# Half-height TensorE tiles, one stretch for four pairs' last queries, and a new order in a funnel-attention and maxout kernel

## The chip, the cores and the metric

The kernel runs on one core of a Trainium2 chip. The metric is device time in microseconds; lower is better. Median of three runs before the change: 359.93 us (359.83 to 361.86).

## The reference

Attention over queries that are averaged in pairs, then a two-branch layer with a maximum:

```python
q_pool = q.reshape(B, H, S // 2, 2, D).mean(axis=3)         # B 8, H 8, S 1152, D 64
scores = scale * q_pool @ k.transpose(0, 1, 3, 2)
attn = exp(scores) / sum(exp(scores))
x = (attn @ v).transpose(0, 2, 1, 3).reshape(B * 576, 512)  # 4608 tokens
g = np.maximum(x @ w1, x @ w2)                              # 512 x 1024 each
out = g @ w_out                                             # 1024 x 512
```

Inputs and output are float32; the kernel multiplies in bf16.

## The kernel before

**The work.** The 64 heads are handled as 32 pairs (`NPAIR`), four to a batch. A pair has 9 x 576 columns of scores per head; all pairs' columns, one after the other, are cut into 324 groups of 512 (`scores`, `exps`). For a group TensorE makes the scores of both heads in 64-row tiles, one in the upper and one in the lower half of the array (line 290), and ScalarE takes the exp of 2 x 512 columns into `et` (line 305; where a group crosses a turn of the buffer, two exps, so 336 in all). K and Q must be transposed first: Q on TensorE (line 491) for pairs 0 to 4, on VectorE (line 446) after that; K on TensorE (line 512) for pairs 0 to 4, by a DMA transpose after that.

Attention times V (`av_jobs`): per head four blocks of 128 queries, each nine matmuls with a 128 x 128 weight tile (line 569), and 64 remaining queries in 128 x 64 tiles (line 584). The 64 of an even pair are copied to `rem` by POOL (`keep_rest`, line 429), so that two pairs' remainders run in one stretch. A column of ones in V yields the sums; VectorE divides (lines 598 to 606). The result x is transposed by DMA, or on TensorE for the pairs in `X_PE` (lines 660 and 663).

The second layer uses max(a, b) = relu(a - b) + b. So x(W1 - W2) goes through a relu (`h_jobs`, line 694; evicted at 705 or 709), and the output is that times Wo plus x(W2 Wo) (`p_job`, line 737; `z_job` at the end). W2 Wo is made once: W2 is cast, transposed on TensorE (`w2t_job`, line 530) and multiplied by Wo (`w21_job`, line 543), both in 128-row tiles. `fill` (line 473) multiplies ones by ones: 28 times before the first data are there, and later two at a time.

**What sets the order.** The order of all instructions is one string, written out: each symbol issues one step. `S` is a group of scores, `E` an exp, `A` a part of attention times V, `Q` and `K` transposes, `T` and `W` W2's transposes and its product with Wo, `X` transposes of x, `0` to `3` four running jobs of the second layer (the sequence `MOE`), `Z` its last rows, `F` two matmuls of ones; small letters are evictions, casts (`k`, `q`, `v`), copies of remainders (`e`), loads (`l`), DMA transposes (`t`, `x`) and stores (`o`). `BANKS` names the PSUM bank of each job. Every engine executes its own steps in the string's order; `Plan` adds the semaphore waits. TensorE's steps thus differ in tile size: 64-row (scores and second layer), 128 x 128 (`A`, `K`, `T`, `W`, `X`, `F`, `Z`), 128 x 64 (remainders), 64 x 64 (`Q`).

SyncE issues nearly all loads in the order `LOADS`, and the DMA transposes and stores between them. q, k and v have three buffers each. From exp 42 on a load also waits until the exp two before the last one issued is done (`pace`).

Of the kernel before, what the change touches and what calls it, by code (L numbers as in the profile page):

```python
# [5 lines left out]
FP32 = mybir.dt.float32  # L6
BF16 = mybir.dt.bfloat16
P = 128
# [108 lines left out]
def bass_funnel_attn__then__act_maxout2_kernel(  # L117
# [38 lines left out]
    W_CASTS = ((0, 1), (0, 2), (0, 0), (0, 3), (2, 0), (2, 1), (2, 2), (2, 3))  # L156
    W_DIFFS = ((0, 0), (0, 1), (3, 1), (1, 1), (1, 0), (3, 0), (2, 1), (2, 0))
    W_DIFFS_DVE = ()
    FILL = 28
    FILLS = 6  # L160
    PACE = 2
    PACE_FROM = 40
    LOADS = (
# [16 lines left out]
        "hhhhpphhhhpphhhhhhhhpphhhhpphhhhphhhhpphhhhphhhhphhhhpphhhhhphhhhphhh"  # L180
    )
    BANKS = (
        "0102346702674670602456042760460245602456012456214624160246246021460234064032646203460426704064036206"
        "2402642604264206250624024624624620742064064060560640640240260246124064024026412640240240240240246246"
        "2562462464267024602462062402462562624640646246246246246206206036026206260202612602402614262642042040"
        "4040645064064062416240204620642642674264240246240634062062462074206406406065060460240240240240202404"
        "2064306426046060467046064060640265026404024024012640260420460142604206406406420101420002406206204232"
# [3 lines left out]
    with ctx:  # L191
# [20 lines left out]
        rc = [sbuf([P, NCH + 2], FP32, f"rc{s}") for s in range(2)]  # L212
# [15 lines left out]
        osb = [osb2[:, s, :] for s in range(4)]  # L228

# [91 lines left out]
        done = [0]  # L321

        def load_k(i, lo=0, hi=NT, eng="SP"):
            b, h0, s = i // NHP, 2 * (i % NHP), i % 3
            op(eng, lambda e: e.dma_start(  # L325
                kraw[s][:, :, lo:hi, :].rearrange("p h t d -> p h (t d)"),
                k[b, h0:h0 + 2, :, :].rearrange("h (p t) d -> p h (t d)", t=NT)[
                    :, :, lo * D:hi * D]),
                after=([f"kraw0.{c}" for c in K0] if s == 0 and hi - lo == NT else []) + pace(),
                w=[f"kraw0.{lo}"] if hi - lo < NT else [f"kraw{s}"],  # L330
                dma=f"d_kp{lo}" if hi - lo < NT else f"d_k{s}",
                cost=1.45 * (hi - lo) / NT + (0.47 if lo == 6 else 0.0), tag=("L", "k", i))

        def load_q(i, lo=0, hi=QU, eng="SP"):
            b, h0, s = i // NHP, 2 * (i % NHP), i % 3
            op(eng, lambda e: e.dma_start(  # L336
# [3 lines left out]
                w=[f"qraw0.{lo}"] if hi - lo < QU else [f"qraw{s}"],  # L340
                after=(["qraw0.0", "qraw0.4"] if s == 0 and hi - lo == QU else []) + pace(),
                dma=f"d_qp{lo}" if hi - lo < QU else f"d_q{s}",
                cost=1.45 * (hi - lo) / QU + (1.1 if lo else 0.0), tag=("L", "q", i))

        def load_v(i):
            b, h0, s = i // NHP, 2 * (i % NHP), i % 3
            op("SP", lambda e: e.dma_start(
                vraw[s][:, :, :, :].rearrange("p h t d -> p h (t d)"),
                v[b, h0:h0 + 2, :, :].rearrange("h (p t) d -> p h (t d)", t=NT)),
                w=[f"vraw{s}"], after=pace(), dma=f"d_v{s}", cost=1.48, tag=("L", "v", i))  # L350

        def w_load(part, c):
            src, dst, name = ((moe_w2, w2f, "w2f"), (moe_w1, w1f, "w1f"), (moe_w_out, wof, "wof"))[part]
            n = 2 if part == 2 else 1
            op("SP", lambda e: e.dma_start(
                dst[:, c * n:(c + 1) * n, :],
                src.rearrange("(c p) f -> p c f", p=P)[:, c * n:(c + 1) * n, :]),
                w=[f"{name}{c}"], dma=f"d_w{part}{c}", cost=1.34, tag=("L", "w", part, c))
# [3 lines left out]
        def setup():  # L362
# [11 lines left out]
            if FILL:  # L374
                op("DVE", lambda e: e.memset(rem[:, 0, :, :], 1.0), w=["rem"], cost=0.1)
                op("PE", lambda e: fill(e, 7, FILL), r=["rem"], w=["b7"], cost=0.0563 * FILL, mode="f",
                   tag=("f0",))
# [37 lines left out]
        def cast_v(i):  # L415
            r = i % 3
            op("POOL", lambda g: g.tensor_scalar(  # L417
                vE[r][:, :, :, 0:D].rearrange("p t h d -> p h t d"), vraw[r][:, :, :, :],
                1.0, 1.0, ALU.mult, ALU.mult), r=[f"vraw{r}"], w=[f"vE{r}", f"v.{i}"], cost=1.154,
                tag=("cv", i))  # L420

        def keep_rest(i):
            a = flat(i, 0, NCH * P)
            step = flat(i, 1, NCH * P) - a
            base = (i % 2) * PW + a
            src = et2[:, :, base:base + NT * step].rearrange("p h (t c) -> p t h c", c=step)[:, :, :, 0:NB] \
                if base + NT * step <= 2 * PW else None
# [546 lines left out]
```

## Time and profile before

| | |
|---|---|
| median of 3 runs | 359.93 us |
| the profiled execution | 360.63 us |
| its span, first to last instruction | 358.9 us |
| TensorE busy | 349.2 us |
| ScalarE busy | 315.3 us, of it exps 303.8 |
| VectorE busy | 236.0 us |
| POOL busy | 143.4 us |
| granted TensorE clock | 1.00 |
| moved by DMA | 84.67 MB, 236 GB/s |

How to read it: PE is TensorE's matmuls, PEld its weight loads, DVE VectorE, ACT ScalarE, SP SyncE. In rows of groups stand line, engine, operation, output <- inputs, shape, count, then busy time in all and the mean of one in ns, then the engine's idle time ahead of them and what ended most of it. In rows in order of time stand start, length, engine, line and, in brackets, the idle time before. Rows of TensorE in order of time overlap, because each matmul's latency is in its length; the distance of two starts is what the first one takes from the stream. A tile is given as rows*columns, so 64*128 is a half-height tile.

### The profile page before, as it was taken

To read this page: it belongs to the slowest core of one execution; us is meant where nothing else is said; L and a number is where in the kernel's file an instruction comes from. 1 tells how busy PE (TensorE), PEld (TensorE's weight loads), DVE (VectorE), ACT (ScalarE), POOL (GpSimd) and SP (SyncE) were. 2 spreads that over 40 slices of the span, in tenths; PEclk is the share of its full clock that TensorE was granted. 3 is DMA by queue.
4 is the path that set the end of the run, shared out by engine and by line. 5 is a ranking of instruction groups with operands and counts; after the bars stand their busy time and mean duration, and the time that the engine had idled before them with its cause. 6 is when DMAs were issued, how large, how long until landed. Compare 5 with 4: busy or idle time off the path is not lost.

```text
span 358.9 us, 13458 instructions
## 1 busy us (share of the span) xinstructions
PE 349.2 (97%) x6009; PEld 218.0 (61%) x6009; DVE 236.0 (66%) x516; ACT 315.3 (88%) x355; POOL 143.4 (40%) x128
## 2 busy tenths in 40 slices
PE   7699999999999999999999999999999999999996
PEld 5465655655566675656664675666676655657663
DVE  3686578977798658976796776884787774514001
ACT  5999989999999989999999898999999898890431
POOL 2446997363645171744417152535425220100000
PEclk9999999999999999999999999999999999999999
DMA  8999999999999999998999989899999853002224
GB/s 264 409 392 395 316 374 257 298 244 291 314 244 315 288 294 297 329 260 148 343 209 301 233 217 305 187 274 255 196 265 228 170 113 75 17 23 59 60 60 117
DMA packets 77434, 84.67 MB, mean 236 GB/s; under 512 B 49216, under 2 KB 50496, under 8 KB 77376
## 3 DMA queue, kind: packets, MB, share of 16 engines
q1 hardware_dynamic: 76592, 83.28, 88.3%
q8 instruction: 47, 0.77, 0.9%
q10 hardware_dynamic: 784, 0.52, 0.5%
q14 instruction: 11, 0.09, 0.1%
HBM read 62.91 MB, written 9.44 MB: 202 GB/s over the span
## 4 chain that ended last, share of the span: by engine, by line
PE 92%; DMA 3%; ACT 2%; SPq 1%; issue 1%; DVE 0%
PE ps L737 25%; PE ps L290 21%; PE ps L569 21%; PE ps L694 18%; PE ps L584 3%; DMA qraw<-in_q_dram 3%; ACT et L305 2%; PE ps L543 2%; PE ps L780 1%; PE ps L660 1%; SPq L325 0%; PE ps L491 0%; PE ps L512 0%; SPq L336 0%; PE ps L663 0%
## 5 line engine op out<-in xcount | busy, mean ns | idle before, releaser
L305 ACT ACTIVATE et<-ps 128x1024 bf16<-128x1024 f32 (+1 forms) x336 | 303.8, 1016 | 14.0 <-PE ps L290 13.1
L290 PE MATMUL ps<-qpT,kT 64*128 64x256 bf16 (+7 forms) x1162 | 114.5, 283 | 1.2 <-DVE qpT L498 0.6
L446 DVE STREAM_TRANSPOSE qpT<-qp 32x288 bf16<-32x288 bf16 x216 | 101.4, 469 | 12.7 <-PE ps L290 6.0
L694 PE MATMUL ps<-xT,wd 64*128 64x512 bf16 (+3 forms) x832 | 84.1, 311 | 0.0
L569 PEld LDWEIGHTS ps<-vE,et 128*128 128x128 bf16 x2304 | 73.6, 97 | 16.9 <-issue 10.0
L569 PE MATMUL ps<-vE,et 128*128 128x65 bf16 x2304 | 81.5, 193 | 1.9 <-issue 1.4
L737 PE MATMUL ps<-wo,stage 64*128 64x512 bf16 x544 | 78.4, 376 | 0.0
L290 PEld LDWEIGHTS ps<-qpT,kT 64*128 64x128 bf16 x1162 | 47.6, 94 | 48.4 <-ACT et L305 15.1
L411 POOL TENSOR_TENSOR qp<-qraw 128x576 bf16<-128x576 f32 x30 | 42.1, 1406 | 53.8 <-DVE qpT L446 48.9
L417 POOL TENSOR_SCALAR vE<-vraw 128x1152 bf16<-128x1152 f32 x32 | 36.9, 1152 | 56.8 <-PE ps L584 39.3
L694 PEld LDWEIGHTS ps<-xT,wd 64*128 64x128 bf16 x832 | 36.0, 94 | 24.5 <-ACT et L305 1.7
L381 POOL TENSOR_SCALAR kbf<-kraw 128x1152 bf16<-128x1152 f32 x31 | 35.7, 1151 | 32.5 <-DMA kraw<-in_k_dram 24.6
L705 DVE TENSOR_SCALAR stage<-ps 128x1024 bf16<-128x1024 f32 (+3 forms) x40 | 39.1, 979 | 13.4 <-PE ps L694 12.7
L737 PE MATMUL ps<-w,xT 64*128 64x512 bf16 x272 | 39.9, 377 | 0.0
L737 PEld LDWEIGHTS ps<-wo,stage 64*128 64x128 bf16 x544 | 25.8, 94 | 18.5
L598 DVE RECIPROCAL rc<-ps 128x4 f32<-128x4 f32 (+1 forms) x64 | 11.8, 184 | 35.5 <-PE ps L569 34.9
L606 DVE TENSOR_TENSOR xnat<-ps,rc 128x256 bf16<-128x256 f32 x64 | 27.2, 424 | 1.9
L429 POOL TENSOR_SCALAR rem<-et 128x1152 bf16<-128x1152 bf16 x16 | 18.4, 1152 | 20.9 <-ACT et L305 20.8
L743 DVE COPY stage<-ps 128x1024 f32<-128x1024 f32 x14 | 17.0, 1216 | 11.6 <-PE ps L737 11.4
L709 ACT ACTIVATE stage<-ps 128x512 bf16<-128x512 f32 (+1 forms) x12 | 6.0, 525 | 17.4 <-PE ps L694 17.4
L785 DVE COPY stage<-ps 128x512 f32<-128x512 f32 (+1 forms) x2 | 1.0, 492 | 25.7 <-PE ps L780 25.7
L737 PEld LDWEIGHTS ps<-w,xT 64*128 64x128 bf16 x272 | 12.6, 94 | 8.5 <-ACT et L305 0.2
(46 smaller groups left out, 138.5 us busy)
## 6 DMA issues: line engine op xcount, KB each, us to landing
vraw<-in_v_dram SPq DMA_DIRECT2D x32, 576.0 KB, 6.1
kraw<-in_k_dram SPq DMA_DIRECT2D x31, 576.0 KB, 7.0
qraw<-in_q_dram SPq DMA_DIRECT2D x31, 576.0 KB, 6.2
out_dram<-stage SPq DMA_DIRECT2D x24, 256.0 KB, 3.8
out_dram<-stage SPq DMA_DIRECT2D x21, 128.0 KB, 3.0
xT<-in_moe_w_dram SPq DMA_DIRECT2D x4, 512.0 KB, 11.2
stage<-in_moe_w_out_dram SPq DMA_DIRECT2D x4, 512.0 KB, 13.6
stage<-in_moe_w_dram SPq DMA_DIRECT2D x4, 512.0 KB, 14.0
```

The lines of the kernel that those rows point to most:

```text
L290: last = e.matmul(ps[:, h, col:col + hi - lo], kT[i % 3][rows(h), t, :], qpT[i % 3][rows(h), lo:hi], start=True, stop=True)
L305: op("ACT", lambda e: e.activation(et2[:, :, c:c + z - a], ps[:, :, a - g * W:z - g * W], EXP, scale=scale), r=[f"b{m}", f"b{m + 1}"], w=w ...
L381: op("POOL", lambda g: g.tensor_scalar(kbf[s][:, :, :, :].rearrange("p t h d -> p h t d"), kraw[r][:, :, :, :], 1.0, 1.0, ALU.mult, ALU.mu ...
L411: op("POOL", lambda g: g.tensor_tensor(qpf[s][:, :, :], qraw[r][:, :, 0, :], qraw[r][:, :, 1, :], ALU.add), r=[f"qraw{r}"], w=[f"qp{s}.0", ...
L417: op("POOL", lambda g: g.tensor_scalar(vE[r][:, :, :, 0:D].rearrange("p t h d -> p h t d"), vraw[r][:, :, :, :], 1.0, 1.0, ALU.mult, ALU.m ...
L429: op("POOL", lambda g: g.tensor_scalar(rem[:, :, :, :], src, 1.0, 1.0, ALU.mult, ALU.mult), r=[f"et{i % 2}.{g - first(i)}" for g in range( ...
L446: op("DVE", lambda e: e.transpose(view[dst:dst + 32, :, 32 * pb:32 * pb + 32], qpf[s][src:src + 32, :, 32 * db:32 * db + 32]), r=[f"qp{s}. ...
L569: last = e.matmul(fb[m][:, sb * 66:sb * 66 + 65], et[:, a:a + P], vE[vs][:, t, half, 0:65], start=(t == 0), stop=(t == NT - 1))
L606: todo.append(evac_op("DVE", lambda e, m: e.tensor_tensor(xnat[xs][:, i % NHP, :, half * D:half * D + D], a(m)[:, 0:NCH, 0:D], rc[half][:, ...
L694: last = e.matmul(fb[m + k][:, 0:size], wd[z, ct, (f0 + k) * P:(f0 + k + 1) * P], xT[z, ct, n0:n1], start=(turn == 0 and ct == 0), stop=(t ...
L705: return e.tensor_scalar_max(gT[:, f0:f0 + 2, g0:g0 + size], wide[m // 2][:, :, 0:size], 0.0)
L737: last = e.matmul(fb[m + k][:, :], lhs, rhs, start=(turn == 0 and j == 0), stop=(turn == 1 and j == NC_ + NF - 1))
```

## The change

- K's transposes of pairs 0 to 4, W2's and those of x on TensorE: each 128 x 128 tile becomes two 64-row transposes in the two halves of the array, into two PSUM banks; the eviction reads both banks. K of pairs 1 to 4 is one job instead of two.
- W2 times Wo: two jobs of two column tiles in 64-row tiles, 64 matmuls of 512 columns in place of 32 in full tiles. They run as the first jobs of the second layer's sequence (`w` in `MOE`), with one eviction each.
- Remainders: from batch 1 on the four pairs of a batch in one stretch (`FOUR`). Three `rem` buffers and a fourth V buffer (in the space of loaded weights that are no longer needed); POOL copies three of four pairs; the last pair's jobs take three and five blocks of 128 queries; VectorE divides four remainders at once; one DMA transpose per four.
- Matmuls of ones: 16 pairs later on in place of 6 (`FILLS`).
- Loads: a new order, and SyncE's loads from the 15th on wait for the landing of the third load before (`BEHIND`).
- The order string, `BANKS`, `MOE` and the order of casts are new.

```diff
-    FILLS = 6
+    FILLS = 16
+    BEHIND = ((14, 3),)
+    FOUR = 1
...
-        ("q", 0, 4, 9), ("k", 1), ("w", 0, 1), ("k", 2), ("q", 1), ("v", 0), ("w", 0, 2), ("w", 0, 0),
-        ("q", 2), ("w", 0, 3), ("q", 3), ("v", 1), ("w", 2, 0), ("w", 2, 1), ("k", 3), ("w", 2, 2),
-        ("w", 2, 3), ("w", 1, 0), ("k", 4), ("q", 4), ("k", 5), ("v", 2), ("v", 3), ("w", 1, 3),
+        ("q", 0, 4, 9), ("k", 1), ("q", 1), ("q", 2), ("k", 2), ("v", 0), ("w", 0, 1), ("w", 0, 3),
+        ("k", 3), ("w", 0, 0), ("w", 0, 2), ("v", 1), ("w", 2, 0), ("w", 2, 1), ("w", 2, 2), ("q", 3),
+        ("w", 2, 3), ("w", 1, 3), ("v", 2), ("w", 1, 2), ("k", 4), ("w", 1, 1), ("q", 4), ("q", 5),
...
+        def behind():
+            n = issued[0]
+            issued[0] += 1
+            back = [d for at, d in BEHIND if at <= n]
+            return [f"ld{n - back[-1]}"] if back else [], [f"ld{n}"]
...
+        def halves(e, m, at, src):
+            for z in range(2):
+                mb = fb[m + z][:, :].bitcast(BF16)
+                last = e.transpose(mb[:, at:at + HP], src[rows(z), :], ident[rows(z), rows(z)])
+            return last
...
-                    last = e.transpose(
-                        mb[:, (t - lo) * P:(t - lo + 1) * P],
-                        kbf[s][:, t, :, :].rearrange("p h d -> p (h d)"), ident[:, :])
+                    last = halves(e, m, (t - lo) * HP, kbf[s][:, t, :, :].rearrange("p h d -> p (h d)"))
...
-                    return e.matmul(fb[m][:, :], w2T[:, ct, ft, :], wo[:, ft, :],
-                                    start=(ft == 0), stop=(ft == NF - 1))
+                    for k in range(2):
+                        z = rows(turn ^ k)
+                        last = e.matmul(fb[m + k][:, :], w2T[z, c0 + k, j, :], wo[z, j, :],
+                                        start=(turn == 0 and j == 0), stop=(turn == 1 and j == NF - 1))
...
+            n = 4 if i // NHP >= FOUR else 2
+            return [i + 1 - n + j for j in range(n)] if i % n == n - 1 else []
...
+            if len(ends) == NHP:
+                return [Job(("a", i, 0), 1, [rest(j, 3 + at) for at, j in enumerate(ends)]
+                            + [chunk(0, sb, sb) for sb in range(3)],
+                            norm(0, 7, [ending(0, 3), ending(1, 3), blocks(0, 0, 0, 3)])),
+                        Job(("a", i, 1), 1, [chunk(0, 3, 0)] + [chunk(1, sb, 1 + sb) for sb in range(NCH)],
+                            norm(1, 5, [blocks(0, 0, 3, 1), blocks(1, 1, 0, NCH)]))]
```

More of the change, by code (lines that the diff above doesn't have):

```diff
@@ new lines, in norm, with blocks, ending @@
+                return todo
+            def blocks(half, at, lo, num):
+                return (slice(0, P), at, num, xnat[xs][:, c, lo:lo + num, half * D:half * D + D],
+                        [f"xn{xs}.{h0 + half}"], 0.154 + 0.068 * num)
+            def ending(k, at):
+                c0 = ends[0] % NHP
+                return (rows(k), at, len(ends), xend[xs][rows(0), c0:c0 + len(ends), k * D:k * D + D],
+                        [f"xr{xs}.{2 * (j % NHP) + k}" for j in ends], 0.154 + 0.068 * len(ends))
@@ new lines, in av_jobs @@
+            if len(ends) == NHP:
[4 more added lines that the diff above has]
+                            norm(1, 5, [blocks(0, 0, 3, 1), blocks(1, 1, 0, NCH)]))]
+            lead = [rest(j, NCH + at) for at, j in enumerate(ends)]
@@ L616, in place @@
+            more = [ending(0, NCH), ending(1, NCH)] if ends else []
+            return [Job(("a", i, half), 1, (lead if half == 0 else [])
+                        + [chunk(half, sb, sb) for sb in range(NCH)],
+                        norm(half, NCH + (len(ends) if half == 0 else 0),
+                             (more if half == 0 else []) + [blocks(half, 0, 0, NCH)]))
+                    for half in range(2)]
         def place(b, j):
```

293 lines of the change are left out of this document (156 added, 137 removed), and 8 rows, old and new, of the table LOADS.

## The prediction

> **What bounds the kernel now.** I read the head of the page first, then the table by stages, then ScalarE's and TensorE's instructions in order of time.
>
> ```profile
> span 358.9 us, 13458 instructions
> PE 349.2 (97%) x6009; PEld 218.0 (61%) x6009; DVE 236.0 (66%) x516; ACT 315.3 (88%) x355; POOL 143.4 (40%) x128
> PE 92%; DMA 3%; ACT 2%; SPq 1%; issue 1%; DVE 0%
> ...
> 10.00:20.00 10.00, 7.46 (x156) 5.55 (x158) 7.77 (x14) 9.68 (x11) 4.93 (x5) 1.00 1.03 408
> 20.00:30.00 10.00, 9.53 (x191) 6.14 (x185) 9.24 (x17) 10.00 (x13) 4.16 (x4) 1.00 1.05 390
> 30.00:40.00 10.00, 9.98 (x118) 4.68 (x118) 4.96 (x12) 10.00 (x12) 8.38 (x7) 1.00 1.04 400
> 80.00:120.00 40.00, 40.00 (x708) 24.35 (x706) 31.06 (x70) 39.80 (x45) 19.31 (x17) 1.00 1.12 286
> 160.00:323.00 163.00, 163.00 (x2858) 101.69 (x2855) 112.24 (x242) 153.75 (x170) 56.63 (x47) 1.00 0.84 199
> ...
> 6.10 6.55 ACT L305 ACTIVATE et<-ps 128x1024 bf16<-128x1024 f32 x7 [0.89 <-PE ps L290]
> 12.88 36.31 ACT L305 ACTIVATE et<-ps 128x1024 bf16<-128x1024 f32 x41 [0.23 <-PE ps L290]
> 50.24 12.20 ACT L305 ACTIVATE et<-ps 128x1024 bf16<-128x1024 f32 x13 [1.05 <-PE ps L290]
> ```
>
> (Columns of the stages: length, busy time of PE, PEld, DVE, ACT, POOL, clock, DMA share, GB/s.) There are two regimes. From 6.10 to 49.2 us ScalarE runs 48 exps with one gap, 0.23 us: it sets the pace, and between 10 and 20 us TensorE is busy only 7.46 of 10. From 50 us on TensorE has no free time (163.00 of 163.00), while ScalarE gets some (153.75). So from exp 48, the 49th, the end is what TensorE still has to do. Ahead of it, shorter TensorE work only makes TensorE wait longer for exps.
>
> **What TensorE pays beside its columns.** The next rows are TensorE's, in the steady part.
>
> ```profile
> 203.07 0.38 PE L290 MATMUL ps<-qpT,kT 64*128 64x512 bf16 x2
> 203.29 1.03 PE L737 MATMUL ps<-wo,stage 64*128 64x512 bf16 x8
> 204.15 0.38 PE L290 MATMUL ps<-qpT,kT 64*128 64x512 bf16 x2
> 204.37 0.59 PE L737 MATMUL ps<-wo,stage 64*128 64x512 bf16 x4
> 204.89 0.47 PE L584 MATMUL ps<-vE,rem 128*64 128x65 bf16 x18
> ...
> 197.65 0.60 PE L290 MATMUL ps<-qpT,kT 64*128 64x128 bf16 x8
> 198.18 2.35 PE L569 MATMUL ps<-vE,et 128*128 128x65 bf16 x72
> 200.46 0.39 PE L290 MATMUL ps<-qpT,kT 64*128 64x256 bf16 x4
> ...
> 53.64 0.40 PE L660 MATMUL ps<-ident,xnat 128*128 128x128 bf16 x4
> 53.97 0.23 PE L663 MATMUL ps<-ident,xend 64*128 64x64 bf16 x2
> ```
>
> I use starts, since ends are pipelined. Where the tile size stays, a pair of 64-row matmuls of 512 columns takes 203.29 - 203.07 = 0.22 us. Four of them at 204.37 should take 0.43, but the next row starts 0.52 later, and its tiles are 128*64: the switch costs 0.09. Eight at 197.65 are two groups, 0.43; the 128*128 row comes 0.53 later: 0.10. Four transposes at 53.64 take 0.33 with their switch. I price a switch at 0.096 us, and the plain rates at 0.216 a 512-column slot, 0.056 a 128*128 transpose and 0.27 a nine-step attention block.
>
> **The change, part by part.** I walked both order strings, gave every TensorE symbol its tile size and counted the changes of size: 205 before, 172 after. That is 33 x 0.096 = 3.17 us less.
>
> ```profile
> L512 PE MATMUL ps<-ident,kbf 128*128 128x128 bf16 x45 | 4.4, 221 | 1.3 <-POOL kbf L381 0.9 <-ACT kbf L394 0.3
> L530 PE MATMUL ps<-ident,xT 128*128 128x128 bf16 x32 | 2.3, 220 | 0.6 <-DVE xT L454 0.6
> L660 PE MATMUL ps<-ident,xnat 128*128 128x128 bf16 x32 | 3.2, 221 | 0.0
> L663 PE MATMUL ps<-ident,xend 64*128 64x64 bf16 x12 | 1.4, 195 | 0.0
> L491 PE MATMUL ps<-ident,qp 64*64 64x64 bf16 x90 | 2.5, 195 | 0.5 <-DVE qp L404 0.5
> L543 PE MATMUL ps<-wo,xT 128*128 128x512 bf16 x32 | 9.0, 382 | 0.0
> 14.36 0.47 PE L491 MATMUL ps<-ident,qp 64*64 64x64 bf16 x18 [0.47 <-DVE qp L404]
> ```
>
> K, W2, x: 45 + 32 + 32 = 109 tiles of 0.056 become 109 pairs of 64-row transposes. No row has such a pair. The nearest, L491's 18 small ones, take 0.47 with 0.195 of latency, so 0.275 / 9 = 0.031 a pair. Bounds: 0.027 (64 columns at the 512-column rate), and 0.060 if the two halves do not overlap, since L569 above loads a full weight tile every (200.46 - 198.18 - 0.096) / 72 = 0.030. I take 0.030: -2.8 us. Eight more 64-query transposes of x on TensorE cost 8 x 0.03 = +0.2. W2 times Wo: 32 slots either way: 0. So TensorE's own work falls by 3.2 + 2.6 = 5.8 us; summed over the whole walk, with a half-tile pair near its lower bound, 334.6 becomes 328.5, 6.1 less.
>
> How much lies behind exp 48? Switches there: 142 before, 110 after, -3.07 us. Six W2Wo slots (6 x 0.216 = 1.30) move ahead of it; two attention blocks (+0.54) and one score group less (-0.21) come behind it; two more x transposes, each cheaper, are even. Sum: -4.0 to -4.1 us. The other 2.0 us, nearly all of the K and W2 transposes, lie where ScalarE sets the pace: worth 0.
>
> ```profile
> L584 PE MATMUL ps<-vE,rem 128*64 128x65 bf16 x288 | 7.6, 197 | 0.0
> L429 POOL TENSOR_SCALAR rem<-et 128x1152 bf16<-128x1152 bf16 x16 | 18.4, 1152 | 20.9 <-ACT et L305 20.8
> L602 DVE TENSOR_TENSOR xend<-ps,rc 64x64 bf16<-64x64 f32 x64 | 14.2, 221 | 1.2
> L519 DVE COPY kT<-ps 128x640 bf16<-128x640 bf16 x4 | 1.9, 483 | 0.5 <-PE ps L512 0.5
> L519 DVE COPY kT<-ps 128x512 bf16<-128x512 bf16 x4 | 1.7, 419 | 1.9 <-PE ps L512 1.9
> L473 PE MATMUL ps<-rem 128*128 128x128 bf16 x40 | 4.5, 290 | 1.1 <-DVE rem L375 1.1
> ```
>
> Last 64 queries of four pairs: as many L584 steps, in 13 stretches instead of 17 (its switches are counted). POOL copies 23 times instead of 16, 7 x 1.152 = 8 us, hidden while POOL is 40% busy. If POOL falls behind, the v cast behind the copy holds up attention. DVE's 64 L602 become 4 of twice and 14 of four times the width: some 5 us less, on no path. SyncE issues seven DMA transposes fewer. The evictions of the half-tiles write two strips: 0 if they keep L519's rate, (483 - 419 ns) / 128 elements by its two sizes; at twice that, nine tiles cost 0.6 us more five times, in a stage where DVE is 9.24 of 10 busy. Ten more pairs of matmuls of ones (20 x 0.056 = 1.1) fall into the idle 2.5 us between 10 and 20: 0; without that cover, 1.1.
>
> ```profile
> kraw<-in_k_dram SPq DMA_DIRECT2D x31, 576.0 KB, 7.0
> qraw<-in_q_dram SPq DMA_DIRECT2D x31, 576.0 KB, 6.2
> 4.20 9.32 DMA qraw<-in_q_dram
> ```
>
> Loads: each SyncE load from the 15th on waits until the one three before it has landed; stores and DMA transposes queue behind that wait. The transfers take 576 KB / 400 GB/s = 1.47 us each, so three cover 4.4 us of latency. At 7.0 us they would not; but the 7.0 contains queueing. I take a latency of 4.4 or less: 0. Weights are also moved ahead of q3 and q4. q1 landed at 4.20 + 9.32 = 13.52 with 3.47 MB through it; 9.57 MB stand up to q3 now, so q3 lands at 13.5 + 6.1 / 0.40 = 28.8, some 3 us of cast, transpose and eviction before its first exp at about 33; q4 10 us later, with some 1.5 us to spare. Pair 1's q comes earlier.
>
> **Sum.** The profiled execution took 360.63 us (span 358.9); the median of the runs shown is 359.93, 0.70 lower. 360.63 - 4.1 = 356.5. ScalarE is then even nearer to full between 50 and 120 (39.80 of 40 already), so I give back 0.2 of the bound of 1.05, the one wait of that kind in the rows: 356.7, or 356.0 as a median.
>
> **The rivals.** *All 6.1 us count,* because the early exps come sooner too: 353.8. For it, ScalarE's one early gap; against it, that gap is only 0.23.
>
> *Loads too late (the other side).* If three in flight take 7.0 us, a load takes 2.33 instead of 1.47: eleven loads from the 15th to q4 lose 9.5 us, less 1.5 to spare, 8.0: 364.0. It takes the whole gain of 4.1 from (4.1 + 1.5) / 11 = 0.51 us more a load, so from 2.0 us a load. For it, the 7.0; against it, that DMA moves 400 GB/s there whatever the queue holds.
>
> *Halves do not overlap:* 109 x 0.060 = 6.5 instead of 6.1 us; 77 of the tiles come early, when TensorE is 9.5 to 10 of 10 busy, so some 2 us: 358.0. [...] No run here shows two half-tile loads back to back.
>
> ```profile
> 10.57 0.68 PE L512 MATMUL ps<-ident,kbf 128*128 128x128 bf16 x9 [0.77 <-POOL kbf L381]
> 1.10 3.38 PE L473 MATMUL ps<-rem 128*128 128x128 bf16 x30 [1.10 <-DVE rem L375]
> ```
>
> *The clock falls.* TensorE idles more between 8 and 17 us, its W2 work being later. The first 30 matmuls of ones ran at (3.38 - 0.29) / 29 = 0.107 us each instead of 0.056. Another such stretch of 3.38 us at half rate costs up to 1.7 us: 357.7. The granted clock was 1.00 with 7.46 of 10 busy and gaps of up to 0.77 us, and the new matmuls of ones are spread over this stretch, which speaks against it. [...]
>
> **How the numbers follow.** My forecast 0.55 (own range 355 to 357.3), all counted 0.14, late loads 0.16, no overlap 0.09, clock 0.06. About 1%, 3.6 us, is what a measurement can tell from no change: faster means below 356.3. That takes 0.33 of my forecast's 0.55 and all of the second: 0.47. Late loads end above 363.5 with 0.12 of their 0.16. The rest, 0.41, is within 1%. The range 353.7 to 361.0 leaves out late loads beyond the point where they decide, and little below.
>
> **What would show it.** Right: switches of tile size down to about 172; row pairs of half-tile transposes starting about 0.03 us apart; ScalarE without gaps up to exp 48 and exp 48 at about 50; TensorE full from 50 us on. Wrong: gaps of ScalarE before exp 48 that end on a DMA or on a q or k cast; a clock below 1.00; transposes 0.06 apart; new TensorE waits after 50 us.

## The result, and the profile after

The changed kernel takes 363.74 us (median of 8 executions, 362.14 to 366.06) against 359.88 for the kernel before (8 executions): a ratio of 1.0089, interval 1.0061 to 1.0117. It is slower by 3.9 us by the medians (3.2 by the ratio) where 3.9 faster was forecast. The profiled execution took 362.49 us. In it, scores are L302 (before L290), exps L317 (L305), half-tile transposes of K, W2 and x L552, the matmuls of ones L515, and h L760; attention is L621 and L636, p is L803.

The head of the page after, and its chain of waits:

```profile
span 360.8 us, 13815 instructions
PE 347.0 (96%) x6178; PEld 218.6 (61%) x6178; DVE 230.0 (64%) x472; ACT 314.0 (87%) x354; POOL 151.7 (42%) x136
PE 76%; DMA 12%; ACT 6%; DVE 2%; SPq 2%; issue 1%; POOL 1%; DVEq 0%; POOLq 0%
```

TensorE is busy for less time than before (347.0 against 349.2), and the span is longer: work has gone and waits have come. In the chain, TensorE falls from 92% to 76% and DMA rises from 3% to 12%. The stages after, in the columns of the prediction's table, show where:

```profile
20.00:30.00 10.00, 8.86 (x214) 5.99 (x215) 8.29 (x11) 9.68 (x12) 1.56 (x2) 1.00 0.89 298
30.00:40.00 10.00, 8.31 (x155) 4.91 (x151) 6.36 (x14) 8.10 (x10) 6.70 (x6) 1.00 0.95 324
40.00:50.00 10.00, 7.76 (x152) 4.53 (x146) 4.39 (x9) 7.70 (x10) 8.42 (x9) 1.00 0.97 327
```

Between 30 and 40 us the DMA engines moved 400 GB/s before and move 324 now, and TensorE and ScalarE, both full before, are at 8.31 and 8.10 of 10. ScalarE's exps in order of time, after:

```profile
5.99 19.43 ACT L317 ACTIVATE et<-ps 128x1024 bf16<-128x1024 f32 x22 [0.78 <-PE ps L552]
25.75 7.44 ACT L317 ACTIVATE et<-ps 128x1024 bf16<-128x1024 f32 x8 [0.32 <-PE ps L302]
35.09 10.21 ACT L317 ACTIVATE et<-ps 128x1024 bf16<-128x1024 f32 x11 [1.91 <-PE ps L302]
47.55 37.31 ACT L317 ACTIVATE et<-ps 128x512 bf16<-128x512 f32 x42 [2.25 <-PE ps L302]
```

The one gap of 0.23 us before exp 48 has become three of 0.32, 1.91 and 2.25. Exp 48 starts at 53.22 us; it was 50.24. These 3.0 us are not made up again: exp 335 is 3.35 late, and the span ends 1.9 late because the tail behind the last exp is 1.5 shorter. The chain of waits says what the gaps stand behind. After, start and length of its pieces:

```profile
19.20 4.54 DMA vraw<-in_v_dram
23.76 5.20 DMA stage<-in_moe_w_out_dram
28.98 5.23 DMA stage<-in_moe_w_dram
34.22 5.14 DMA kraw<-in_k_dram
39.38 5.37 DMA qraw<-in_q_dram
44.82 1.41 POOL qp L435
```

Each load is issued about 0.02 us after the landing of the one before it in this list: they are loads three apart, and the limit of three under way ties them to one another. Three loads in some 5.2 us are 1.73 us a load.

Two things behind these gaps are easily misread. The gap of 2.25 us ends behind the load of q5, not of q4, which landed 1.7 us before it: VectorE transposes q5 (at 46.26) ahead of the copy of q4 that the scores wait for. And the gap of 1.91 us stands behind a weight, the last quarter of Wo, which landed at 32.92 us; q3 had landed at 30.45. VectorE prepares that quarter, and TensorE multiplies it ahead of the scores of exp 30:

```profile
32.95 1.22 DVE L498 TENSOR_REDUCE wo<-stage 128x1024 bf16<-128x1024 f32 x1 [1.57 <-DMA stage<-in_moe_w_out_dram]
34.22 0.61 PE L593 MATMUL ps<-wo,xT 64*128 64x512 bf16 x4 [1.68 <-DVE wo L498]
```

### The profile page after: what moved, and what is told of

Read it like the earlier page. It is cut to its first block, busy times and chain, and to the rows that moved or that the text cites. A ratio compares the mean times of both kernels' runs of the same rounds, so it can differ in the third digit from the quotient of the medians.

```text
span 360.8 us, 13815 instructions
## 1 busy us (share of the span) xinstructions
PE 347.0 (96%) x6178; PEld 218.6 (61%) x6178; DVE 230.0 (64%) x472; ACT 314.0 (87%) x354; POOL 151.7 (42%) x136
## 4 chain that ended last, share of the span: by engine, by line
PE 76%; DMA 12%; ACT 6%; DVE 2%; SPq 2%; issue 1%; POOL 1%; DVEq 0%; POOLq 0%
PE ps L803 23%; PE ps L621 17%; PE ps L302 16%; PE ps L760 15%; ACT et L317 6%; DMA kraw<-in_k_dram 5%; DMA qraw<-in_q_dram 3%; PE ps L636 3%; PE ps L846 1%; DMA stage<-in_moe_w_dram 1%; DMA stage<-in_moe_w_out_dram 1%; DMA vraw<-in_v_dram 1%; DVE qpT L485 1%; POOL qp L435 1%; SPq L346 1%
## 5 line engine op out<-in xcount | busy, mean ns | idle before, releaser
L317 ACT ACTIVATE et<-ps 128x1024 bf16<-128x1024 f32 (+1 forms) x336 | 302.5, 1019 | 18.6 <-PE ps L302 14.1
L302 PE MATMUL ps<-qpT,kT 64*128 64x256 bf16 (+7 forms) x1162 | 117.5, 283 | 4.8 <-DVE qpT L540 1.7
L760 PE MATMUL ps<-xT,wd 64*128 64x512 bf16 (+3 forms) x832 | 81.2, 311 | 0.2
L302 PEld LDWEIGHTS ps<-qpT,kT 64*128 64x128 bf16 x1162 | 48.2, 94 | 52.4 <-ACT et L317 10.7
L803 PE MATMUL ps<-wo,stage 64*128 64x512 bf16 x544 | 76.4, 376 | 0.0
L435 POOL TENSOR_TENSOR qp<-qraw 128x576 bf16<-128x576 f32 x30 | 42.2, 1406 | 67.5 <-DMA qraw<-in_q_dram 67.5
L621 PEld LDWEIGHTS ps<-vE,et 128*128 128x128 bf16 x1728 | 54.8, 97 | 13.7 <-ACT et L317 8.9
L621 PE MATMUL ps<-vE,et 128*128 128x65 bf16 x1728 | 60.5, 193 | 0.5 <-ACT et L317 0.3
L760 PEld LDWEIGHTS ps<-xT,wd 64*128 64x128 bf16 x832 | 35.6, 94 | 22.3 <-PE ps L760 1.9
L803 PE MATMUL ps<-w,xT 64*128 64x512 bf16 x272 | 40.8, 377 | 0.0
L803 PEld LDWEIGHTS ps<-wo,stage 64*128 64x128 bf16 x544 | 26.4, 94 | 20.6
L445 POOL TENSOR_SCALAR vE<-vraw 128x1152 bf16<-128x1152 f32 x24 | 27.4, 1154 | 21.4 <-PE ps L636 10.7
L654 DVE TENSOR_TENSOR xnat<-ps,rc 128x256 bf16<-128x256 f32 (+2 forms) x71 | 27.6, 397 | 2.0
L651 DVE RECIPROCAL rc<-ps 128x4 f32<-128x4 f32 (+2 forms) x64 | 11.6, 181 | 25.8 <-PE ps L621 25.2
L468 POOL TENSOR_SCALAR stage<-et 128x1152 bf16<-128x1152 bf16 x14 | 16.1, 1153 | 28.1 <-ACT et L317 28.1
L621 PE MATMUL ps<-stage,et 128*128 128x65 bf16 x576 | 19.8, 193 | 0.4 <-issue 0.4
L621 PEld LDWEIGHTS ps<-stage,et 128*128 128x128 bf16 x576 | 18.2, 97 | 3.2 <-issue 3.1
L803 PEld LDWEIGHTS ps<-w,xT 64*128 64x128 bf16 x272 | 12.5, 94 | 8.8 <-DVE stage L771 0.2
```

Of the source, the lines that this page charges most:

```text
L302: last = e.matmul(ps[:, h, col:col + hi - lo], kT[i % 3][rows(h), t, :], qpT[i % 3][rows(h), lo:hi], start=True, stop=True)
L317: op("ACT", lambda e: e.activation(et2[:, :, c:c + z - a], ps[:, :, a - g * W:z - g * W], EXP, scale=scale), r=[f"b{m}", f"b{m + 1}"], w=w ...
L435: op("POOL", lambda g: g.tensor_tensor(qpf[s][:, :, :], qraw[r][:, :, 0, :], qraw[r][:, :, 1, :], ALU.add), r=[f"qraw{r}"], w=[f"qp{s}.0", ...
L445: return g.tensor_scalar(vE[r][:, :, :, 0:D].rearrange("p t h d -> p h t d"), vraw[s][:, :, :, :], 1.0, 1.0, ALU.mult, ALU.mult)
L621: last = e.matmul(fb[m][:, at * 66:at * 66 + 65], et[:, a:a + P], vE[vs][:, t, half, 0:65], start=(t == 0), stop=(t == NT - 1))
L654: todo.append(evac_op("DVE", lambda e, m, z=z, at=at, num=num, dst=dst: e.tensor_tensor(dst, a(m)[z, at:at + num, 0:D], rc[k][z, at:at + n ...
```

## What the runs told apart

My theory after the two traces was that the limit on loads (BEHIND) costs DMA throughput and that this alone makes the loss; the rivals were that the new order puts q too late in the queue whatever the limit, and that the loads only uncover a cost elsewhere. All ratios below are to the kernel before, on the same chip, with a 95% interval.

**The limit.** The edits, of which only the last is made to the kernel before (with the function `behind` and its calls from the diff):

```
e1  -    BEHIND = ((14, 3),)      +    BEHIND = ()
e2  -    BEHIND = ((14, 3),)      +    BEHIND = ((14, 4),)
e3  -    BEHIND = ((14, 3),)      +    BEHIND = ((14, 3), (40, 999))
e4  before                        +    BEHIND = ((14, 3),)
```

> The changed kernel with BEHIND empty: no load waits for an earlier one to land, all else as changed. Theory A (the cap of three loads in flight costs bandwidth: 5.2 us from issue to landing over three loads is 1.73 us a load, against 1.45 where the queue was full, so q3, q4 and the weights come up to 4.4 us late): loads 14 to 27 land 1.45 us apart again, q4 lands near 39 us, the exps' gaps of 1.91 us (exp 30) and 2.25 us (exp 41) shrink below 0.5 each, and the time is 357.5 to 359. Theory B (the new order of the loads is at fault, weights ahead of q3 and q4): both gaps stay above 1 us, and the time is 361 or more. Theory C (the cap is there to keep DMA transposes quick): the first transpose of K lands later than 53 us and new gaps stand after exp 48; time 361 or more.

> The changed kernel with a cap of four loads in flight instead of three. Theory A: four loads cover 4 x 1.45 = 5.8 us, more than the 5.2 us from issue to landing, so the rate is full again and the time is that of the run without a cap within 0.5 us. Theory B and C: 361 or more, the gaps at exps 30 and 41 as with three.

> The changed kernel with the cap of three for the loads 14 to 39 alone and none from the 40th on. Theory A: all of the loss is made between 20 and 55 us, so the time is that of the changed kernel, 362 to 364. A rival to it (the cap also holds loads back later, where DMA transposes and stores share the queue): 360 or less.

> The kernel before with the cap of three added and nothing else. In its order q3 and q4 are the 14th and the 23rd load, so at 1.73 us a load q4 lands 9 x 0.28 = 2.5 us later, near 37 us, and is needed at about 41. Theory A with the order as a condition: no gap before exp 48 above 0.5 us, time 359.5 to 361. If the cap alone is enough to lose time whatever the order: 362 or more.

Measured: without the limit 358.55 us, 0.9958 (0.9927 to 0.9988). With four under way 360.17, 0.9990 (0.9958 to 1.0021). With three, only up to load 40, 364.18, 1.0100 (1.0064 to 1.0136). The kernel before with the limit 366.21, 1.0160 (1.0120 to 1.0201). So the limit alone costs some 5 us, in the old order as in the new (4.7 and 5.8 by the ratios); the old order was expected to bear it, and does not. Lifting the limit from load 40 on, which is issued at 69 us, gains nothing, so the loss is made before that. In the new order it is complete at exp 48. In the old one exp 48 is 2.8 us late and exp 80 5.3; between them TensorE waits 0.9 us for a v at 60 us and 1.4 for a DMA transpose of K at 68.

Four under way were expected to be as good as no limit, within 0.5 us, and are 1.2 to 1.6 us slower, with intervals that overlap. In that run a load takes 5.4 to 6.6 us, and loads come every 1.49 us. The stages of the run without the limit (e1):

```profile
30.00:40.00 10.00, 10.00 (x173) 5.78 (x171) 5.50 (x10) 9.52 (x11) 8.75 (x8) 1.00 1.04 403
40.00:50.00 10.00, 9.99 (x231) 6.65 (x226) 7.84 (x17) 9.97 (x13) 9.80 (x10) 1.00 0.96 282
```

TensorE is full again, at 403 GB/s, and the exps before the 48th have one gap, of 0.27 us: the new order does not put q too late by itself. Load 13 lands at 22.2 and load 26 at 40.5 us, 1.40 a load; with the limit at 22.3 and 44.8. q4 lands at 39.05 without it and at 43.04 with it, q5 at 40.48 and 44.75, and exp 48 starts at 49.35 against 53.22: these loads are 4.0 and 4.3 us late, and the exps 3.9. With four under way q4 lands at 40.23, and exp 48 starts at 50.15.

**Where the rest of the gain is.** The run without the limit gains 1.5 us, not 4. First I suspected an engine that hides it: ScalarE or the loads as the bound, or the pacing of loads behind exps (PACE). The edits:

```
e5  e1 and  -    PACE = 2                   +    PACE = 0
e6  e1 and  -    for i, t, lo, hi, col in pieces(g):
            +    for i, t, lo, hi, col in list(pieces(g)) * (2 if 56 <= g < 120 and g % 4 == 0 else 1):
e7  before, with the edit of e6
e8  e1, with K and W2 transposed in tiles of 128 rows again (x as in the change)
```

In e6 and e7, sixteen score groups between 56 and 119 are computed twice, which adds 3.4 us of TensorE work and changes no value.

> The changed kernel without the cap and without the pace (from exp 42 on a load waits for no exp). The run without the cap took 358.55 us, some 2 to 3 us more than the sum of the prediction. Theory D (between exp 48 and exp 160 the loads of q and v, issued no earlier than the pace lets them, set the end beside the exps): with loads sent as soon as their buffers are free the time is 356 to 357.5. Theory E (in that stretch ScalarE's own exps are the bound, loads are not): 358 to 359.5, unchanged. A rival to both (a full queue of loads delays the DMA transposes behind it): 360 or more.

> The changed kernel without the cap, with 16 groups of scores between groups 56 and 119 computed twice (3.4 us more TensorE work, nothing else; the second pass overwrites the first with the same values). If TensorE is the bound there, as the prediction had it: +3.4 us, about 362. If ScalarE's exps or loads are the bound in that stretch (theories D and E), part of it is hidden: +0.5 to +2 us, about 359 to 360.5.

> The kernel before with the same 16 groups of scores computed twice (3.4 us more TensorE work). There TensorE has next to no waits between 50 and 120 us, so every theory expects most of it to show: +2.5 to +3.4 us over the kernel before.

> The changed kernel without the cap, with the transposes of K and W2 in 128-row tiles again (77 tiles at 0.056 instead of 0.030 us, four more switches: 2.4 us more TensorE work, all before exp 48; banks and order as changed). The prediction's step that this work is worth nothing, because ScalarE sets the pace there: 358 to 359.5, as without the cap. If TensorE is the bound early too: 360.5 to 361.

Measured: without pacing 0.9956 (0.9930 to 0.9981), no change. Doubled groups 1.0080 (1.0055 to 1.0106) in the new order and 1.0106 (1.0078 to 1.0135) in the old. The added work costs 1.2% or 4.4 us over e1 in the one and 3.8 in the other: both agree with the 3.4 within their intervals. TensorE is the bound in both, and nothing hides its work there. Full-height transposes 1.0001 (0.9984 to 1.0019), 1.4 to 1.5 us over e1: some 2.0 us of work (77 tiles by 0.026) and four switches, most of it in the stage where the prediction took such work to be worth nothing. This edit also moves all later code by 77 matmuls, which matters below, so the 1.5 is a bound and no price.

If TensorE is the bound and its work fell, it must stand still somewhere else. I took its instruction starts, gave each form its plain time and each switch 0.096 us, and called the rest a stall. In us:

| | plain work | 172 or 205 switches | stalls | of these, 30 to 60 us | 60 to 130 us |
|---|---|---|---|---|---|
| before | 321.5 | 19.7 | 13.3 | 2.1 | 0.4 |
| after | 319.8 | 16.5 | 19.9 | 5.9 | 2.9 |
| no limit, second run (below) | 319.8 | 16.5 | 16.6 | 2.2 | 3.3 |

Work and switches fell by 4.9, with the 1.1 of matmuls of ones in it. Without the limit 3.3 us come back as stalls, 2.9 of them between 60 and 130 us. The second figure hangs on what is taken as a form's plain time: with the median distance of starts it is 1.9, while the 3.3 becomes 3.2.

**Are the loads just in time?** In the new order a q load stands on average 5.9 exps ahead of its cast in the order string (8.4 before), a k load 6.9 (8.5), and GpSimd waits 67.5 us for q where it waited 4.8. So I moved the load symbols only: e9 is e1 with all loads from pair 6 on at least nine exps ahead (v eight), e10 with q alone, and e11 the kernel before with q at most six and k at most seven ahead.

> The changed kernel without the limit on loads under way (as in the first run, 358.55 us), and with every load from pair 6 on put earlier in the order string: k and q loads at least nine exp steps ahead of the cast that reads them (7 and 6 on average in the changed kernel, 8.5 and 8.4 in the kernel before), v loads at least eight. Nothing else moves. Theory F, that the new order puts its loads too close to their casts (a load takes 5 to 7 us from issue to landing, six exps are 5.5 us, and GpSimd stands 67 us waiting for q in the changed profile against 5 before), says that this is where the rest of the forecast gain went: 356 to 357.5 us, and GpSimd's wait for the q load falls from tens of us to below 15. Rival G, that the leads cost nothing on the path, and that the gain is spent on waits for instructions, on the order of 128-column jobs and on early TensorE work that was never a saving: 358 to 359 us although GpSimd's wait falls. Rival H, that earlier loads stand in the queue ahead of the transposes by DMA and hold those up: over 359.5 us.

> As the run with all loads earlier, but only the q loads are moved (at least nine exp steps ahead of the cast; k and v where the changed kernel has them). Theory F with the q chain (load, GpSimd cast, VectorE transposes, VectorE's queue behind them) as its path: within 0.5 us of the run with all loads earlier, 356 to 357.5 us. F with k as the late one: between that and 358.5 us. Rival G: 358 to 359 us.

> The kernel before, with its q and k loads from pair 6 on put later in the order string: q at most six exp steps ahead of its cast and k at most seven (8.4 and 8.5 on average before), which are the leads of the changed kernel; v stays. Theory F: 1.5 to 3 us over the kernel before, since the loads land just as their casts want them, and GpSimd's wait for q goes from 5 us to some tens. Rival G: within 0.6 us of the kernel before, although GpSimd waits.

Measured: 0.9979 (0.9947 to 1.0011), 0.9988 (0.9963 to 1.0013), and 1.0035 (1.0008 to 1.0062). The longest wait of GpSimd for a load in e9, and then TensorE's waits there between 50 and 330 us (us in all, times, longest):

```profile
POOL qp L533 <- DMA qraw<-in_q_dram: 33.0, 12, 5.4
```

```profile
PE ps L719 <- POOL vE L543: 1.7, 1, 1.7
PE ps L400 <- issue: 1.4, 1, 1.4
PE ps L719 <- issue: 1.0, 1, 1.0
```

GpSimd's wait was halved, not brought below 15 as expected, and nothing was won; one v load, now behind more q and k loads, comes late at 60 us. The theory falls as the main cause: late leads cost the old order about 1.2 us, between what the theory and its rival expected, but taking them away does not give the new order its gain. What is left in these profiles, as in those of the changed kernel and of e1, is a wait of the kind in the second row: TensorE stands still with no semaphore to wait for.

**The code of TensorE.** In e1, TensorE in order of time:

```profile
89.08 1.80 PE L621 MATMUL ps<-stage,et 128*128 128x65 bf16 x54
90.82 0.39 PE L302 MATMUL ps<-qpT,kT 64*128 64x64 bf16 x4
93.15 0.61 PE L302 MATMUL ps<-qpT,kT 64*128 64x128 bf16 x8 [1.94 <-issue]
```

The page's DMA queues of e1 (queue and kind: packets, MB, share of the 16 engines) have beside the data:

```profile
q8 instruction: 48, 0.79, 0.9%
```

That is 16 KB a packet. The 0.79 MB are 64 bytes for each of TensorE's 2 x 6178 matmuls and weight loads, and one packet comes per 128 pairs. The kernel before has 47 packets for 6009 pairs, and the run with 60 more pairs (e12, below) 49 for 6238: this is TensorE's own code. The packet before the row at 93.15 ran from 90.91 to 91.87 us; TensorE stood from 91.21 on. Counting back 128 pairs from where TensorE ran dry, a packet lands in these traces some 3 to 4 us later at the median and 5 to 6 at worst. The stretch of 128 pairs that ends at 93 us takes 4.7 us without its gap: 54 pairs of attention at 0.030 us each, and more such before them, use up code faster than anything else near it. In the old order these blocks are spread differently; its two stalls of this kind, at 47 and 136 us, sum to 1.4 us.

Three more runs test this: 60 more pairs ahead of 35 us, five fewer, and e1 repeated as a partner (e14).

```
e12  e1 and  -    last = e.matmul(fb[m][:, 0:P], one, one, start=True, stop=True)
             +    for lo, hi in zip(cuts, cuts[1:]):
             +        last = e.matmul(fb[m][:, lo:hi], one, one[:, lo:hi], start=True, stop=True)
     with cuts = (0, 64, 128)
e13  e1 and  -    FILL = 28                  +    FILL = 23
```

> The changed kernel without the limit on loads, with the same work and the same order, but 60 more matmul and weight-load pairs in the first 35 us: each of the 28 fills at the start and of the 32 fills in the order is issued as two matmuls of 64 columns in place of one of 128, the same columns in all. TensorE's code comes in pieces of 16 KB, one for each 128 pairs (48 transfers on the instruction queue for 6178 pairs), and by the traces so far a piece lands 3.7 us after the pair that seems to ask for it, at the median, and up to 5 to 6 us at worst. Theory I: TensorE stands idle where its 128 pairs take less than that, so the places of the stalls follow the count of pairs. The stretch of 128 pairs that ends at the stall near 92 us takes 4.8 us without its gap, the shortest of the kernel before 285 us or so; shifted by 60 pairs it takes 5.1, and the shortest become 3.75 us at 288, 3.9 at 212, 4.3 at 133 and 4.6 at 171. So: no stall at 92, stalls for no visible reason near 133, 171, 212 or 288, and 1.5 to 4 us over the repeat of the kernel without the limit. Rival J, that these stalls belong to the place in the work or to the traffic there: the stall at 92 stays, and the time is within 0.7 us of the repeat.

> The changed kernel without the limit on loads, with 23 fills at the start in place of 28, so that the boundaries of TensorE's pieces of code move by five pairs the other way. Theory I: the sum by which its stretches of 128 pairs are shorter than 5.3 us is 1.1 us in place of 1.8, so -0.3 to -0.8 us against the repeat. Rival J: no change, within 0.3 us.

> The changed kernel without the limit on loads once more, on the chip of the two runs with shifted code, so that they have a partner there. Both theories: 358 to 359.5 us and a ratio of 0.994 to 0.998, as in the first run.

Measured: repeat 358.83 us, 0.9966 (0.9941 to 0.9991); 60 more pairs 360.56, 1.0007 (0.9979 to 1.0035); five fewer 359.82, 0.9983 (0.9955 to 1.0011). TensorE's waits between 40 and 330 us, in the repeat and with 60 more pairs:

```profile
PE ps L302 <- issue: 1.1, 1, 1.1
PE ps L302 <- DVE stage L809: 0.5, 2, 0.2
PE ps L621 <- ACT et L317: 0.3, 1, 0.3
```

```profile
PE ps L553 <- issue: 1.3, 1, 1.3
PE ps L637 <- issue: 0.7, 1, 0.7
```

With 60 more pairs the stall at 92 us is gone, and TensorE stands 1.3 us at 51.5 and 0.7 at 285: same work, same order, another place. With five fewer the stall at 92 stayed, and there is one of 1.5 us at 284.

The profiles of all runs, taken together, settle what the places follow. They have 30 gaps of TensorE of over 0.3 us that end on "issue", and each ends 1.2 to 1.6 us after the end of a 16 KB packet of this queue. Counted in matmuls from the first, the gaps stand behind 474, 729, 984, 1620, 2258 or 2259, 2385, 3535, 4682, 4934 and 5062 of them, whole multiples of about 127.4 apart, in both orders. With five matmuls fewer ahead, the gaps still stand behind 1620 and 5062, which is five matmuls further on in the work, and with 60 more still one behind 5062. So these stalls go with the count of instructions. Rival J, the place in the work, falls.

The 1.7 us more of e12 is inside what was expected of it. But of the four places expected only 285 came, and 51.5, which was not among them, stalled first. The length of the stretch therefore makes a stall possible and does not decide it; how late the packet is, which the traffic may set, was not controlled. The gain expected of five fewer did not come; the stall at 284, and a clock that opened 5 us later in that profile (below), could hide an effect of this size.

**The clock.** The mean clock of a run is listed with its time. In the first eight executions of the changed kernel it was 0.995 or less in five, and those took 364.24 at the median, the three others 362.49. It was so in eight of nine executions of e3, but in only 7 of 124 of the kernel before, one of six of e4 and 2 of 24 of e1 and e14 (seven of 24 in e9 and e10). So I took the last part of the change that had not been run alone (e15: e1 with the last ten matmuls of ones in the order left out, as many left as before), and two more profiles of the changed kernel.

```
e15  e1 and  -    FILLS = 16                 +    FILLS = 6
     and the last ten F of the order string with their banks
```

> The changed kernel without the limit on loads and without the last ten of its sixteen pairs of fill matmuls (the six first ones stay, as many as the kernel before has): 1.1 us less TensorE work, all of it before 15 us. It is the part of the change that has not been run by itself. If the fills only fill gaps: within 0.6 us of the kernel without the limit (358.5 to 359 us, ratio 0.9958 to 0.9966). If they keep the granted clock up: a stretch at half clock in the first 30 us, 1 to 2 us more. If they stand in the way of other work: up to 0.7 us less. It moves TensorE's code by 20 pairs as well, which by the sum over stretches of 128 pairs would cost 0.5 to 1 us.

> The changed kernel itself, to see with a profile one of its executions with a granted clock of 0.995 or less (five of its first eight, and eight of nine of the run with the limit up to load 40; seven of 107 of the kernel before and one in ten of the new order without a limit). Those took 1.7 us more than the others at the median. Theory K, that a gap of TensorE of over a microsecond is followed by some 3.4 us at half clock, as in the profiles with the code piece late at 91 and at 51 us: a stretch at 0.5 behind one of the gaps that the limit makes between 30 and 48 us, and a span 1.5 to 2 us over the 360.8 of the first profile, all of it lost there. Rival: the clock falls late in the kernel, in the stretch of full work, and has nothing to do with the gaps.

> The same as the look before it, a second chance of a profile with a lowered clock.

Measured: e15 359.33 us, 0.9984 (0.9963 to 1.0005), with a lowered clock in six of twelve executions, which are no slower than the other six (359.2 against 359.8 at the median). The two further profiles took 363.91 (clock 1.000) and 363.54 us (0.995). The stages of the second of them, around the lowered clock:

```profile
31.77:35.18 3.41, 1.39 (x28) 0.70 (x27) 1.66 (x4) 1.62 (x2) 0.89 (x2) 1.00 0.95 318
35.19:38.60 3.41, 3.41 (x42) 1.91 (x40) 0.85 (x3) 2.11 (x3) 3.41 (x4) 0.52 0.84 266
38.60:42.01 3.41, 3.41 (x76) 2.29 (x71) 2.47 (x4) 2.96 (x4) 2.28 (x3) 0.98 0.99 348
```

Read the first busy time of a row (PE) and its clock, the third number from the end. Behind a stretch in which TensorE worked 1.39 of 3.41 us comes one at half clock, and then full clock again. It is where the late loads leave TensorE idle, as the theory of the run said. The same pair of rows in e1, behind its late packet of code, and with 60 more pairs, behind that one's:

```profile
90.88:94.30 3.42, 1.48 (x38) 1.10 (x38) 2.15 (x7) 2.10 (x3) 3.21 (x3) 1.00 1.37 282
94.30:97.71 3.41, 3.41 (x43) 2.26 (x41) 2.72 (x8) 2.24 (x3) 1.15 (x1) 0.52 0.90 269
```

```profile
50.53:53.94 3.41, 1.83 (x48) 1.19 (x45) 1.82 (x6) 2.98 (x4) 3.41 (x4) 1.00 1.15 208
53.95:57.36 3.41, 3.41 (x32) 2.16 (x30) 1.88 (x6) 2.08 (x3) 2.86 (x3) 0.52 1.10 336
```

Each such stretch lasts 3.413 us and can cost half of it, 1.7 us. What it did cost can be read in two places. e1 and e14 are the same program, and their profiles are level up to exp 90. At exp 95 e1 is 0.86 us behind, since its gap is 1.94 us and not 1.09; at exp 100 it is 2.39 behind: the half clock adds 1.5, and gap and clock together cost some 3.5. In the changed kernel the profile with the stretch starts exp 48 0.9 us later than the first one and ends 1.0 later, where 1.5 to 2 was expected. The two medians above differ by 1.7 (364.24 - 362.49); with the two further profiles counted it is 1.0 (364.1 of six, 363.1 of four).

## Why the prediction was wrong, point by point

**The loads: the step that failed.** "At 7.0 us they would not; but the 7.0 contains queueing. I take a latency of 4.4 or less: 0." With three loads under way a load takes 5.2 us and not 4.4. That is 1.73 us a load instead of 1.40, and over the thirteen loads up to q5 4.2 us. The 4.4 had no margin in the profile before either: seven loads issued there between 59 and 78 us, with one to three under way, took 4.1 to 5.4. The arrival times themselves were right for a full queue: q3 at 28.8 and q4 10 us later were forecast, and without the limit they land at 29.4 and 39.05. But the spare time was not there: the sum gave q4 1.5 us, and with four under way, when q4 is 1.2 us late, exp 48 is 0.8 late. The sum also looked at q3 and q4 alone, and the first large gap came behind Wo.

The rival "loads too late" was the right one, with the wrong price. It had the whole gain taken only from 2.0 us a load on, and its own formula gives a loss of 1.4 us at 1.73 (11 x 0.26 - 1.5); it was 3.9 at exp 48. That its 364.0 lies so near the measured 363.74 is luck, since it stands for 2.33 us a load. Its own evidence against, that DMA moves 400 GB/s "whatever the queue holds", came from stages in which the queue is never short: the loads there took 10 to 16 us.

**Less work on TensorE: right.** 172 switches were forecast and are there. Half-tiles overlap; the changed kernel has, in order of time:

```profile
96.82 0.30 PE L552 MATMUL ps<-ident,xnat 64*128 64x64 bf16 x8
96.93 0.28 PE L730 MATMUL ps<-ident,xend 64*128 64x64 bf16 x4
```

Four pairs start within 0.11 us, 0.028 a pair, against 0.060 had each half been loaded in turn, as the rival had it. Here the measurement decides: a pair of 64-row loads takes no longer than one full tile took in the kernel before (0.030 us, L569). Work and switches fell by 4.9 in the profiles, 6.0 without the added matmuls of ones; 5.8 to 6.1 was forecast.

**"Worth 0" ahead of exp 48: wrong, as far as one pair of profiles tells.** Without the limit exp 48 comes 0.9 us earlier than before, and full-height transposes cost 1.1 to 1.5 us, though ScalarE was thought to set the pace there. The profile with them (e8) and that of e13, both without the limit, start exp 20 at 25.72 us; e8 then starts exp 48 at 51.14 and e13 at 50.12. So 1.0 us of this work and of its evictions shows before exp 48. As e8 moves the code too, the price of the whole stays open.

**-4.0 to -4.1 behind exp 48: the work is right, the time is not.** The doubled groups cost their full time, so work there counts. But 1.9 to 2.9 us came back as stalls from 60 to 130 us, where the forecast had 0.2. In the repeat, 1.3 of these are a late packet of code at 92 us and 0.8 are scores that wait behind VectorE's queue near 118 and 128 us; the rest is in pieces of under 0.2. Another 0.9 goes just behind, in the h jobs of 128 columns, of which the order now runs several back to back (the old order lost 0.7 at 136 us, to a packet of code):

```profile
131.44 0.38 PE L302 MATMUL ps<-qpT,kT 64*128 64x384 bf16 x4
131.66 1.31 PE L760 MATMUL ps<-xT,wd 64*128 64x128 bf16 x24
132.81 0.38 PE L302 MATMUL ps<-qpT,kT 64*128 64x448 bf16 x4
```

Twelve pairs of 128 columns are 0.65 us at the plain rate; the next scores start 1.15 after them. There are four such pauses, of 0.17 to 0.23 us, up to 135 us. This list is read from one trace; only the code was tried by experiment, VectorE's queue and the h jobs were not.

**The clock: right that it can fall, wrong in place and weight.** The rival was a half-rate stretch between 8 and 17 us, with a chance of 0.06. In the one profile that shows such a stretch it lies between 35 and 39, behind the gaps that the limit makes; by the mean clock over half of the executions have one or two. Its 1.7 us is the most it can cost; in that profile it was 1.0. It is the second part of the loss: 1.2 to 1.5 gained by order and tiles, 3.9 lost by the limit at exp 48 and some 1.0 by the clock give 363.3 to 363.6, near the median of 363.74. The old order loses its 5.8 us to the limit with a lowered clock in one execution of six, so the clock is not needed for the loss.

**The ten more matmuls of ones: open.** In the stretch from 6 to 17 us, first in the repeat of e1, then in e15, which lacks them:

```profile
L302 PE MATMUL ps<-qpT,kT 64*128 64x256 bf16 x28 | 2.7, 274 | 0.7 <-DVE qpT L540 0.4 <-DVE kT L568 0.2
```

```profile
L301 PE MATMUL ps<-qpT,kT 64*128 64x256 bf16 x24 | 3.4, 408 | 0.4 <-DVE qpT L539 0.4
```

The same scores take 408 instead of 274 ns: by these lengths that execution was still at half clock through this stretch, up to 17 us. One profile does not make a rule, though: in six other profiles the full clock began as late as 9.5 to 13.1 us. A lowered clock came in 6 of 12 executions instead of 2 of 24, but those six are no slower. Without the ten the kernel is 0.6 to 0.9 us slower by the ratios, with intervals that overlap. Part of that may be code again, which they move by 20 pairs: the profile of e15 stands 1.24 us at 31 us, behind 474 matmuls. That the ten cost 0, as forecast, is neither shown nor refuted.

**The rest.** GpSimd's further copies and VectorE's savings were off the path, as forecast. The price of evicting two strips stays open: in the changed profile scores wait 0.7 us for two such evictions of K, at 15.9 and 23.0 us, and 0.2 in the repeat of e1.

The best version measured is the changed kernel without the limit, at 0.9958 and 0.9966 (0.9956 without pacing too): 0.3 to 0.4% faster than the kernel before, and 1.2 to 1.3% faster than the changed one.

## What to carry to other kernels

A transfer time read from a full queue said nothing here of a queue kept short on purpose (1.40 us a load with the queue full in e1, 1.73 with three under way): before limiting what is under way, take the latency that loads have where as few are under way, with its scatter, and check the spacing that follows against what every consumer needs, the weights' too. When work is taken off the engine that sets the end, follow its stalls as well as its work, its own code among them: long runs of the shortest instructions outran the packets that bring them here (1.94 us of stall in e1, behind 54 pairs of 0.030 us). And a gap on TensorE cost its own length here (0.86 us behind for a gap 0.85 us longer, e1 against e14) plus, in the three profiles where it left a window of 3.413 us little more than a third full, a window at half clock: 1.5 us more in e1, 1.0 in the changed kernel.

## What the hardware showed beyond that

In these traces the clock changes in steps of 3.413 us: its stretches are whole numbers of such windows, up to the last one (354.99 us of full clock in the kernel before are 104). In the three traces with a lowered clock it falls 9, 13 and 26 such windows after it first rose (at 35.2 us in the second further profile of the changed kernel, 53.9 in e12, 94.3 in e1), for exactly one window each, at a granted clock of 0.50 (0.52 over the rows above, whose ends are rounded). I counted TensorE's share of work per window from the plain times of its matmuls: the windows ahead of the three falls had 0.34, 0.37 and 0.36; the emptiest without a fall had 0.43 (kernel before, at 8 us, and the changed kernel's first profile, at 22 us). In that first profile the window at 32 us, where the later one was at 0.34, was about half full, and there was no fall. Whether there is a border between 0.37 and 0.43, and the same one everywhere, no run tells.

The start differs between executions of one kernel too: the full clock began at 4.8 us in one profile of the changed kernel and at 10.3 in another, and exp 20 was then 1.3 us later. At exp 48, behind the late loads, the two were level again (53.22 and 53.24). Without the limit, e13, with its clock at 10.5 us, is still 0.8 us behind e14 at exp 48. Part of the scatter between executions may be this.
